# Attention rows turned by VectorE squares and DRAM instead of TensorE, and one table for the order of all later steps

## The chip, the cores and the metric

The kernel runs on one core of a Trainium2 chip. Its time is the device time of one execution in microseconds; the profile is one more execution, taken by the hardware profiler. TensorE (PE) multiplies, VectorE (DVE), ScalarE (ACT) and GpSimd (POOL) work on tiles, and all transfers are issued by SyncE (SP) to 16 DMA engines.

## What is computed

Four batches of attention with a band of 16 keys and 24 block summaries, and behind it a mixing step over the sequence and a gate of two dense layers:

```python
k_sum = k.reshape(B, H, nb, block, D).max(axis=3)      # block 32
v_sum = v.reshape(B, H, nb, block, D).mean(axis=3)
scores = concat(where(|i - j| < 16, scale * q @ k.T, -1e9), scale * q @ k_sum.T + log(block))
x = softmax(scores) @ concat(v, v_sum)                 # B, S=768, 8 heads of 64 -> 512 channels
u = x + (x.T @ U @ V).T                                # U: 768 x 32, V: 32 x 768
out = u + maximum(u @ w_ch1, 0) @ w_ch2                # 512 -> 2048 -> 512
```

## The kernel before

All products of the gate are made in three terms of high and low halves (`split`: ScalarE writes the high half, another engine the remainder). The batches are numbered 0 to 3 in the code, and the text follows that: what the title of the change calls batch 2 is index 1.

**Start.** `START` is a list of words; each is one step (a load, scores, exponentials, a turn, a value product, a mixing product). It brings batch 0's attention to the first gate product.

**Batch 0's gate** runs over f = 0..15 and two halves hf of the sequence: `up` (12 matmuls into `ps_h`, L1071), `up_out` (ScalarE writes the high half `gh`, L1083, VectorE the low half `gl`, L1084), and `down_rows` of the half before (9 matmuls into `acc`, L1093). Six PSUM banks hold `acc`; the two that are left go round between `ps_h` and everything else, so a product waits until the tile before the last has been read out. Beside it the weights come in as 64-bit floats and are converted (`turn_weights`: GpSimd L171, VectorE L177 and L180), split, summed (L923 to L927, L1050 to L1054) and stored to DRAM for the later batches. The attention of batch 1 is spread evenly over the half steps by `places`: scores (L365), masking with the row maximum on VectorE (L414) and the exponential on ScalarE (L424), `turn_half` (three transposes on TensorE into `ps_t`, L499, and a copy by ScalarE, L493), value products (`square_values`, L529), `normalise` (L541 to L543), and the mixing (`mix`, `mix_back`). `operands` then makes the seven operands of the gate: for batch 1 `mix_u` transposes the rows on TensorE (L748) and adds the mixing product in PSUM (L756); ScalarE keeps a copy.

**Batches 1 and 2** run an `up_phase` (eight p with seven products of six matmuls, L1366, after Strassen and Winograd) and a `down_phase` (16 gates f, 24 matmuls each, L1471), with `gate_high` and `gate_low` (L1439, L1443) one gate ahead. The attention of the next batch is spread over both. For batches 2 and 3 the exponentials are turned in another way: `turn_squares` (VectorE transposes 32 by 32 squares, L444), `send_squares` to DRAM (L449) and `fetch_squares` back in four loads (L457); likewise `turn_rows`, `send_rows`, `fetch_rows` for the rows (L469, L473, L482), with `add_rows` (L764, L767) in the place of `mix_u`.

**Batch 3** runs `up_phase` and `second_phase` (L1584). Weights of the later batches come back from DRAM (`fetch_weight`) and are split by `prepare` (L195 ScalarE, L196 GpSimd) right behind the product that used a unit, four units ahead. Steps of a counter (`tick`), of a queue (`drip`) and of `spread` set when each of the rest is issued.

Of the kernel before, what the change touches and what calls it, by code (L numbers as in the profile page):

```python
# [10 lines left out]
F32 = mybir.dt.float32  # L11
# [7 lines left out]
P = 128  # L19
# [16 lines left out]
VALS = 8  # L36
RING = 5
# [18 lines left out]
LEAD = 20  # L56
POOL_LOWS = ()
VALS_LENT = 6
PARTS_IN = {1: (), 2: tuple(range(NF // 2))}
AHEAD_UNITS = (45, 50)  # L60
EARLY = {7 * p + 3 : p for p in range(8)} | {7 * p + 8 : 8 + p for p in range(7)}
EARLY |= {7 * p + 13 : 16 + p for p in range(4)}
FIRST_OPERANDS = [EARLY[i] for i in sorted(EARLY)]
TURNED = {7 * p + 12 : p for p in range(6)}
# [8 lines left out]

START = """
    lm lk0 lq0 lk3 lu li lq3 X K0 Kd0 S0 K3 Kd3 E1 lk2 Xt0 lk1 S3 E0 K2 lq2 E7 Kp2 lq1 S2 E6 T6 E4
    K1 T1 F Xt1 T0 T4 Kp1 lv0 lv1 C0 lk5 S1 C6 lk6 E5 T5 lq5 E2 C1 M0 E3 T7 K5 Xt2 T2 Kp5 Mo0 Bp3 T3  # L90
    Bd2 Xs lq6 K6 C2 Dp0 C4 Dp3 lk4 Bp1 Dp1 C5 Kd6 S5 C7 V1 lk7 V4 lq4 Bp0 C3 Dp2 E10 E11 S6 V2 Xl
    K4 E12 V0 lq7 V5 V7 V3 lv2 lv3 Kp4 K7 Kp7 z0 z1 E13 S4 N1 E8 T10 V6 E9 la0 S7 T11 N2 E14 T12 la3
    T13 Q1 E15 N0 M1 Mo1 C11 N3 Bp5 I0 Bd6 T8 la1 Dd5 lr Z0 Io0 C10 Dp4 T15 lb0 Y0.0 T9 Y0.1 Bp4 Dp7
    C8 T14 V10 V11 Y0.2 C9 Dp6 la4 C14 V9 C13 Bp7 C12 N5 V8 V12 C15 N4 V13 V15 V14 N6 J0 Z1 lb1 Q0
    N7 Jo0 I2 Qo0 lb2 Io2 Y1.0 G0.0 Qo1 J2 G1.0 Y1.1 lb4 G0.1 G1.1 Go0.0 Jo2 G0.2 G0.3 W0 Go0.1
    Go1.1 G1.3 Go0.2 Go0.3 Y1.2 Go1.3 G1.2 Go1.0 Go1.2 W1 lb3 U0.0 la2 Z2
# [8 lines left out]
def body(ctx: ExitStack, tc, q0, q1, k, v, vn, uv, w1, w2, mask, ident, rep, out):  # L105
# [54 lines left out]
    def from_f64(parts, by_pool=False):  # L160

        todo = []
        for words in parts:
            n = words.shape[1] // 2
            pairs = words.rearrange("p (n w) -> p n w", w=2)
            val = mo.tile([P, DM], F32, name="val", tag="val", bufs=VALS)[:, :n]
            todo.append((pairs[:, :, 0], pairs[:, :, 1], val.bitcast(I32), val))
# [16 lines left out]
        for step in steps:  # L184
            for lo, hi, bits, _ in todo:
                step(lo, hi, bits)
                yield
        return [val for _, _, _, val in todo]
# [13 lines left out]
    def new_batch(b):  # L202
# [4 lines left out]
        st.op, st.tmp, st.h, st.rows = ({} for _ in range(4))  # L207
# [112 lines left out]
    def key_maxima(st, h):  # L320
        block_maxima(st, h)

# [1486 lines left out]
```

## Time and profile before

| | us |
|---|---|
| median of three runs | 641.9 (640.96 to 641.91) |
| the profiled execution | 636.64 |
| its span, first to last instruction | 634.7 |
| TensorE busy | 614.0 (97%) |
| VectorE busy | 443.2 (70%) |
| ScalarE, GpSimd busy | 364.0, 346.0 |
| moved by DMA | 138.46 MB |

The granted TensorE clock is 1.0 throughout. Some matmuls have two records, so counts of matmuls in the trace can be twice those in the code. A busy TensorE is modelled at the ends of matmuls, so the chain of waits is read beside it. Windows of time are used for the share of each engine in a stretch, since the stretches have different limits: start (0 to 49 us), batch 0's gate (49 to 218), batch 1's (218 to 368), batch 2's (368 to 514.5), batch 3's.

### The profile page before, as it was taken

What the parts mean: (1) busy time and instruction counts of PE and PEld (TensorE: products, weight loads), DVE (VectorE), ACT (ScalarE), POOL (GpSimd) and SP (SyncE); (2) the same over time, 40 slices, a digit from 0 to 9 for tenths busy, and PEclk for the clock granted to TensorE, in tenths of its full rate; (3) what the DMA queues carried; (4) which work ended last, traced back from release to release, by engine and by line L of the source; (5) the groups of instructions that cost most, each with busy time, mean ns of one, the idle gap of its engine ahead of it and who ended that gap; (6) DMA issues with size and microseconds to landing.
All of it is one profiled execution on the core that took longest, in us unless ns stands there. A gap on an engine that the chain in (4) does not pass through costs nothing.

```text
span 634.7 us, 14717 instructions
## 1 busy us (share of the span) xinstructions
PE 614.0 (97%) x5432; PEld 559.1 (88%) x5432; DVE 443.2 (70%) x1154; ACT 364.0 (57%) x820; POOL 346.0 (55%) x375
## 2 busy tenths in 40 slices
PE   4989999999999999999999999999999999999997
PEld 3778988889888899998888799998888889999997
DVE  4879878776888596667655764566655666756896
ACT  3865666666564556765644456675544447754552
POOL 3525977975685795782328586684134566750000
PEclk9999999999999999999999999999999999999999
DMA  9898599877687459987876366889989454366432
GB/s 235 217 385 260 161 311 295 251 235 238 177 251 216 149 156 290 266 242 241 228 235 173 103 220 181 273 249 322 278 271 270 116 179 146 117 221 235 125 119 88
DMA packets 88199, 138.46 MB, mean 218 GB/s; under 512 B 8512, under 2 KB 60096, under 8 KB 88128
## 3 DMA queue, kind: packets, MB, share of 16 engines
q1 hardware_dynamic: 88128, 137.53, 70.7%
q8 instruction: 43, 0.70, 0.5%
q14 instruction: 28, 0.23, 0.1%
HBM read 99.75 MB, written 37.75 MB: 217 GB/s over the span
## 4 chain that ended last, share of the span: by engine, by line
PE 86%; DVE 6%; SPq 2%; ACT 2%; DMA 2%; issue 2%; POOL 0%; ACTq 0%; DVEq 0%; POOLq 0%
PE ps_h L1366 27%; PE acc L1471 20%; PE acc L1093 9%; PE ps_h L1071 8%; PE accx L1584 4%; PE ps_x L529 3%; PE accy L1584 3%; PE accz L1584 3%; PE ps_s L388 2%; PE ps_s L365 2%; PE ps_t L499 2%; SPq L231 1%; DVE tmp L824 1%; DMA place<-in_v 1%; PE ps_m L714 1%
## 5 line engine op out<-in xcount | busy, mean ns | idle before, releaser
L196 POOL TENSOR_TENSOR parts<-whole,parts 128x512 fp32r<-128x512 f32 (+1 forms) x128 | 161.5, 1273 | 116.0 <-ACT parts L195 110.6
L1366 PE MATMUL ps_h<-place,parts 128*128 128x384 f32 x1008 | 181.6, 337 | 0.1
L1366 PEld LDWEIGHTS ps_h<-place,parts 128*128 128x128 f32 x1008 | 174.2, 188 | 2.5 <-issue 1.1
L1471 PE MATMUL acc<-gh,parts 128*128 128x256 f32 (+1 forms) x512 | 135.1, 342 | 0.0
L1471 PEld LDWEIGHTS acc<-gh,parts 128*128 128x128 f32 x512 | 88.9, 189 | 12.7 <-issue 1.7
L1471 PE MATMUL acc<-gl,parts 128*128 128x512 f32 (+1 forms) x256 | 86.7, 339 | 2.6 <-DVE gl L1443 2.6
L195 ACT CAST parts<-whole 128x512 fp32r<-128x512 f32 (+1 forms) x144 | 83.2, 583 | 4.1 <-issue 1.8
L424 ACT ACTIVATE e<-e,neg 128x120 f32<-128x120 f32 x144 | 46.5, 386 | 52.5 <-DVE neg L414 48.0
L1071 PE MATMUL ps_h<-place 128*128 128x384 f32 x384 | 74.6, 343 | 0.0
L1071 PEld LDWEIGHTS ps_h<-place 128*128 128x128 f32 x384 | 66.3, 188 | 1.5 <-issue 0.4
L1093 PE MATMUL acc<-place,gh 128*128 128x512 f32 x192 | 67.1, 404 | 0.0
L171 POOL TENSOR_SCALAR val<-place 128x512 f32<-128x512 f32 (+1 forms) x30 | 49.4, 1664 | 25.7 <-DMA kt<-in_k 13.3
L1471 PEld LDWEIGHTS acc<-gl,parts 128*128 128x128 f32 x256 | 48.5, 189 | 7.4 <-DVE gl L1443 3.2
L196 POOL TENSOR_TENSOR place<-val,place 128x512 fp32r<-128x512 f32 x29 | 40.6, 1419 | 17.2 <-ACT place L195 17.2
L812 POOL TENSOR_TENSOR place<-tmp,place 128x384 fp32r<-128x384 f32 x24 | 27.2, 1142 | 40.5 <-ACT place L808 35.7
L1443 DVE SCALAR_TENSOR_TENSOR gl<-place,gh 128x768 fp32r<-128x768 f32 x32 | 35.9, 1121 | 17.3 <-ACT gh L1439 16.9
L1439 ACT ACTIVATE gh<-place 128x768 fp32r<-128x768 f32 x32 | 27.0, 844 | 28.7 <-PE acc L1471 28.7
L1093 PEld LDWEIGHTS acc<-place,gh 128*128 128x128 f32 x192 | 36.1, 188 | 7.2
L414 DVE CUSTOM_DVE_ANT_0 e<-ps_s,mask_sb 128x120 f32<-128x120 f32 x144 | 32.8, 277 | 8.3 <-PE ps_s L388 5.3
L1093 PE MATMUL acc<-place,gl 128*128 128x512 f32 x96 | 37.7, 393 | 0.1
L1084 DVE SCALAR_TENSOR_TENSOR gl<-ps_h,gh 128x384 fp32r<-128x384 f32 x32 | 17.7, 554 | 23.8 <-ACT gh L1083 23.7
L1395 DVE TENSOR_TENSOR place<-place,ps_h 128x384 f32<-128x384 f32 x24 | 13.2, 551 | 30.3 <-PE ps_h L1366 30.2
(158 smaller groups left out, 1055.0 us busy)
## 6 DMA issues: line engine op xcount, KB each, us to landing
place<-in_w SPq DMA_DIRECT2D x32, 512.0 KB, 5.6
whole<-up SPq DMA_DIRECT2D x24, 512.0 KB, 4.6
whole<-up SPq DMA_DIRECT2D x24, 384.0 KB, 3.5
whole<-down SPq DMA_DIRECT2D x16, 512.0 KB, 4.8
vt<-in_v SPq DMA_DIRECT2D x48, 146.2 KB, 4.1
kt<-in_k SPq DMA_DIRECT2D x24, 288.0 KB, 5.5
there<-squares SPq DMA_DIRECT2D x16, 384.0 KB, 4.5
at<-there SPq DMA_DIRECT2D x64, 96.0 KB, 3.9
```

Source lines behind the costliest of these rows:

```text
L171: nc.gpsimd.tensor_scalar(f32(bits), f32(hi), 0.0, None, ALU.mult)
L195: nc.scalar.copy(hi, val)
L196: engine.tensor_tensor(lo, val, f32(hi), ALU.subtract)
L414: nc.vector.tensor_tensor_reduce(out=e[:, u, :], in0=ps[:, i * KC : (i + 1) * KC], in1=mask_sb[:, m, :], scale=-SCALE, scalar=BIG, op0=ALU ...
L424: nc.scalar.activation(e[:, u, :], e[:, u, :], AF.Exp, bias=st.neg[h][:, u : u + 1], scale=-1.0,)
L812: engine.tensor_tensor(by_tiles(t[:, 1]), by_tiles(val), by_tiles(f32(t[:, 0])), ALU.subtract)
L1071: nc.tensor.matmul(ps[:, :NH], w_split[0, f][:, c % 2, part_w, c // 2], ut[c], start=(n == 0), stop=(n == 3 * NC - 1),)
L1093: nc.tensor.matmul(acc[t], gt[:, sl], w_split[1, f][:, part_w], start=(first and j == 0), stop=(last and j == 2),)
L1366: nc.tensor.matmul(ps, a[:, sa, i], b[i][:, sb], start=(first and n == 0), stop=(n == 5), skip_group_check=not first,)
L1443: nc.vector.scalar_tensor_tensor(gl, h, 0.0, f32(gh), ALU.max, ALU.subtract)
L1471: nc.tensor.matmul(place, w[:, part_w, c * P : (c + 1) * P], gt[:, q0:q1], start=(f == 0 and i == 0 and j == 0), stop=(f == NF - 1 and j = ...
L1584: nc.tensor.matmul(ps, w[j][:, sa, c * P : (c + 1) * P], gate[sb], start=fresh and q == 0 and j == 0 and k == 0, stop=q == 3 and j == 1 an ...
```

## The change

Three things.

**1. Batch 1's exponentials** are no longer turned by `turn_half` but as those of batches 2 and 3: `turn_squares`, `send_squares`, `fetch_squares`. Its scores stay as they are. **2. Its rows** are turned by `turn_rows`, sent and fetched, and `operands` adds the mixing product with `add_rows`, in place (`turned = c in st.rows`). **3. The order** of all steps behind the start is read from a table, `PLAN`, which takes the place of `START`, `places`, `later`, `traffic`, `spread`, `tick` and `drip`. The table has 481 pieces, one for each point behind a group of products; a word names a step and its batch (`S1.0.1`: batch 1, head 0, bank 1 of scores; `E1.0.1.0`: masking and exponential of one tile; `T`, `s`, `f`: turn, send and fetch of a head's squares; `p0`, `p1`: ScalarE's and GpSimd's half of the next weight unit; `h`, `y`: high and low half of a gate). Steps that were one call are split into single instructions, so that the halves of `prepare`, the six maskings of a head and the parts of `operands` have places of their own. The order of the words of the start is kept, with a few words of later work put between them.

```diff
-START = """
-    lm lk0 lq0 lk3 lu li lq3 X K0 Kd0 S0 K3 Kd3 E1 lk2 Xt0 lk1 S3 E0 K2 lq2 E7 Kp2 lq1 S2 E6 T6 E4
...
+PLAN = """
+    .lm .lk0 .lq0 .lk3 .lu .li .lq3 .X .K0 .Kd0 .S0 .K3 .Kd3 .E1.0 .E1.1 .E1.2 .lk2 .Xt0 .lk1
...
+    l1.1.0 / / / v1.0 S1.0.1 E1.0.1.0 / a1.0.1 S1.0.0 d0.0 c1.3 K1.1 a1.0.1 E1.0.1.1 E1.0.1.2 t4
...
-    def turn_half(st, h, a):
-
-        transposes(st, h, a)
+    def turn_half_out(st, h, a):
+
...
-        if st.b == 1:
+        turned = c in st.rows
+        if not turned:
             mix_u(st, hf, c)
             val = st.ps_u.pop((hf, c))[:, :NH]
         else:
             add_rows(st, hf, c, kept)
             val = kept
+        if k == 0:
+            st.tmp["B12", i] = kept
+        yield
...
-        split(hi, lo, whole, nc.vector if key[0] == "second" else nc.gpsimd)
+        nc.scalar.copy(hi, whole)
         prepared.append((key, t))
...
+        def rest():
+            (nc.vector if key[0] == "second" else nc.gpsimd).tensor_tensor(lo, whole, f32(hi), ALU.subtract)
+            yield
+
+        split_next.append(rest())
...
+    plan = iter(PLAN.strip().split("/"))
+
+    def go():
+        for word in next(plan).split():
+            name = word.rstrip("0123456789.")
+            words_of[name](*map(int, filter(None, word[len(name) :].split("."))))
+
+    go()
...
             g = first.pop() if first else up_out(up(st, hf, f))
-            place(4 * f + 2 * hf)
-            traffic(f, 2 * hf)
...
+            go()
```

How the instructions of three places stand before and after. (Line numbers move with the code: L499 is gone from these places, L365 is now L452, L1071 is L1018, L1093 is L1040, L414 is L500, L1084 is L1031, L1443 is L1364, L824 is L758, L767 is L696.)

TensorE in batch 0's gate, around the product of f = 2, half 1; `ps_t<-ident_sb,e` are the transposes of batch 1's exponentials. Before:

```order
L1093 MATMUL acc_1084<-place,gl 128x512
L1093 MATMUL acc_1084<-place,gh 128x512
L499 MATMUL ps_t<-ident_sb,e 120x128 x3
L1071 MATMUL ps_h<-place 128x384 x12
L365 MATMUL ps_s<-kt,qz_85 128x120 x3
L1093 MATMUL acc_1030<-place,gh 128x512
L1093 MATMUL acc_1030<-place,gl 128x512
```

After:

```order
L1040 MATMUL acc_1098<-place,gl 128x512
L1040 MATMUL acc_1098<-place,gh 128x512
L452 MATMUL ps_s<-kt,qz_85 128x120 x3
L1018 MATMUL ps_h<-place 128x384 x12
L1040 MATMUL acc_1044<-place,gh 128x512
L1040 MATMUL acc_1044<-place,gl 128x512
```

The three transposes are gone, and scores stand where they stood.

VectorE at batch 1's first scores (`e,neg<-ps_s`: masking; `x<-val`: sums of weights; `km`: key maxima; `val`: conversion of weights). Before:

```order
L1050 TENSOR_TENSOR x<-val 128x256
L1051 TENSOR_TENSOR x<-x,val 128x256
L330 TENSOR_REDUCE km<-kt 128x3x2 x2
L177 SCALAR_TENSOR_TENSOR val<-place,val 128x512
L1084 SCALAR_TENSOR_TENSOR gl<-ps_h,gh 128x384
L414 ISA e,neg<-ps_s,mask_sb 128x120
L414 ISA neg 128x1
```

After:

```order
L272 SCALAR_TENSOR_TENSOR val<-place,val 128x512 x2
L269 SCALAR_TENSOR_TENSOR val<-place,val 128x512 x2
L1031 SCALAR_TENSOR_TENSOR gl<-ps_h,gh 128x384 x2
L500 ISA e,neg<-ps_s,mask_sb 128x120
L500 ISA neg 128x1
L997 TENSOR_TENSOR x<-val 128x256
L998 TENSOR_TENSOR x<-x,val 128x256
L417 TENSOR_REDUCE km<-kt 128x3x2 x2
```

Two low halves stand behind six conversions, and the sums and maxima have moved between the first masking of the bank and its two others, which follow right behind.

VectorE at the end of batch 1's down products; `gl` is the low half of the last gate, `x` the rows, `tmp` and `place` the operand sums of batch 2. Before:

```order
L767 TENSOR_TENSOR x_3640<-ps_u_5036,place_4818 128x3x128
L824 TENSOR_TENSOR tmp_5041<-x_3640 128x384
L824 TENSOR_TENSOR tmp_5042<-tmp_5012,x_3640 128x384
L812 TENSOR_TENSOR place_5039<-x_3640,place_5039 128x384
L1443 SCALAR_TENSOR_TENSOR gl_5053<-place_3972,gh_5052 128x768
```

After:

```order
L500 ISA e_5062,neg_5041<-ps_s_5042,mask_sb_78 128x120
L758 TENSOR_TENSOR tmp_5068<-x_3864 128x384
L500 ISA e_5062,neg_5041<-ps_s_5043,mask_sb_78 128x120
L758 TENSOR_TENSOR tmp_5077<-x_3864 128x384
L1364 SCALAR_TENSOR_TENSOR gl_5024<-place_3944,gh_5023 128x768
L758 TENSOR_TENSOR tmp_5086<-tmp_5068,x_3864 128x384
```

The four additions of rows now stand ahead of these rows, and the third operand sum behind the low half.

## Rows read from the trace of the kernel before

**Rows 1.** Page: span, and busy us (share) xinstructions of each engine.

```profile
span 634.7 us, 14717 instructions
...
PE 614.0 (97%) x5432; PEld 559.1 (88%) x5432; DVE 443.2 (70%) x1154; ACT 364.0 (57%) x820; POOL 346.0 (55%) x375
```

**Rows 2.** Chain that ended last, 64 to 92 us: start us, us, what.

```profile
66.73 0.66 PE ps_s L365 x6
67.39 2.11 PE ps_h L1071 x12
69.50 0.33 PE ps_t L499 x3
69.83 2.08 PE acc L1093 x9
```

**Rows 3.** TensorE's waits: engine line waited for: us in total, times, longest us.

```profile
PE acc L1471 <- DVE gl L1443: 2.6, 2, 1.3
...
PE ps_s L365 <- ACT kt L347: 1.3, 1, 1.3
...
PE ps_t L499 <- DVE place L812: 0.9, 1, 0.9
```

**Rows 4.** Windows: busy us (x instructions) of each engine, PEclk, DMA share, GB/s.

```profile
64.00:100.00 36.00, 36.00 (x249) 32.63 (x249) 29.32 (x81) 24.13 (x61) 30.19 (x31) 1.00 0.78 245
100.00:140.00 40.00, 40.00 (x350) 35.35 (x348) 30.59 (x89) 25.39 (x62) 31.65 (x33) 1.00 0.84 265
140.00:180.00 40.00, 39.11 (x278) 34.97 (x278) 32.39 (x69) 24.14 (x55) 26.53 (x19) 1.00 0.71 224
180.00:218.00 38.00, 37.53 (x344) 32.35 (x344) 29.42 (x60) 19.94 (x42) 25.93 (x23) 1.00 0.61 186
```

**Rows 5.** TensorE in order of time, 196 to 245 us, and the chain there.

```profile
205.33 0.33 PE ps_u L748 x3
...
218.25 3.31 PE L1366 MATMUL ps_h<-place,parts 128*128 128x384 f32 x18
```

**Rows 6.** Groups of VectorE: busy us, mean ns | idle before, releaser.

```profile
L444 DVE STREAM_TRANSPOSE squares<-e 128x768 f32<-128x768 f32 x16 | 15.5, 970 | 0.0
...
L767 DVE TENSOR_TENSOR x<-ps_u,place 128x384 f32<-128x384 f32 x16 | 8.9, 555 | 14.4 <-PE ps_u L764 14.3
```

**Rows 7.** VectorE in order of time, 354 to 370 us: start us, us.

```profile
356.26 0.56 DVE L824 TENSOR_TENSOR tmp<-x 128x384 f32<-128x384 f32 x1
...
358.56 1.57 DVE L824 TENSOR_TENSOR tmp<-x 128x384 f32<-128x384 f32 x1
```

**Rows 8.** Groups of VectorE between 64 and 218 us.

```profile
L1084 DVE SCALAR_TENSOR_TENSOR gl<-ps_h,gh 128x384 fp32r<-128x384 f32 x29 | 16.1, 555 | 23.8 <-ACT gh L1083 23.7
...
L414 DVE CUSTOM_DVE_ANT_0 e<-ps_s,mask_sb 128x120 f32<-128x120 f32 x48 | 10.9, 277 | 2.9 <-PE ps_s L365 2.9
...
L414 DVE DVE_READ_ACCUMULATOR2_ANT neg<- 128x1 f32 x48 | 4.0, 83 | 0.0
...
L330 DVE TENSOR_REDUCE km<-kt 128x6 f32<-128x192 f32 x16 | 4.8, 344 | 0.0
...
L1051 DVE TENSOR_TENSOR x<-x,val 128x256 f32<-128x256 f32 x7 | 4.8, 683 | 0.2
...
L1050 DVE TENSOR_TENSOR x<-val 128x256 f32<-128x256 f32 x7 | 3.3, 475 | 0.0
```

**Rows 9.** Groups of ScalarE.

```profile
L1083 ACT ACTIVATE gh<-ps_h 128x384 fp32r<-128x384 f32 x32 | 15.7, 491 | 30.5 <-PE ps_h L1071 30.3
```

**Rows 10.** DMA issues: queue, op xcount, KB each, median us to landing.

```profile
there<-squares SPq DMA_DIRECT2D x16, 384.0 KB, 4.5
at<-there SPq DMA_DIRECT2D x64, 96.0 KB, 3.9
```

**Rows 11.** Page, costliest groups: the low halves of weight units.

```profile
L196 POOL TENSOR_TENSOR parts<-whole,parts 128x512 fp32r<-128x512 f32 (+1 forms) x128 | 161.5, 1273 | 116.0 <-ACT parts L195 110.6 <-PE ps_h L1366 4.4
```

More of the change, by code (lines that the diff above doesn't have):

```diff
@@ L538, in normalise @@
     def normalise(st, h):
+        if not hasattr(st, "x"):
+            st.x = mo.tile([P, NU, DM], F32, name="x")
         ps = st.psx.pop(h)[:, : NU * DV].rearrange("p (u d) -> p u d", d=DV)
@@ L817, in part @@
             high(name, val)
-            low(name, val, nc.gpsimd)
+            yield
+            low(name, val, lows_by[0])
+            yield
         def tmp():
@@ L829, in operands @@
         if k == 0:
-            keep()
-            st.tmp["B12"] = kept
+            if not turned:
+                keep()
+                yield
             return
@@ L877, in scale_weights, with turned_weights, got @@
             scale_f64(words[i, f])
+    def turned_weights(k):
+        turn = turn_weights(k, True)
+        n = 3 * len(tiles(k))
+        for i in range(n):
+            next(turn)
+            if i == n - 1:
+                run(turn)
+            yield
     def turn_weights(k, by_pool=False):
-        vals = yield from from_f64([words.pop(t) for t in tiles(k)], by_pool)
-        for t, val in zip(tiles(k), vals):
-            w_val[t] = val
+        def got(vals):
+            for (i, f), val in zip(tiles(k), vals):
+                w_val[i, f] = w_kept[("down", f) if i else f] = val
+        yield from from_f64([lambda t=t: words[t] for t in tiles(k)], by_pool, got)
     def by_parts(val):
@@ L1591, in second_phase @@
                     )
+            if q == 3:
+                second_out(st, i, n, c, ps)
             yield
-            for more in range(2):
-                lead = (20 if i % 2 == 0 else -1, 6)[more]
-                while st.order and st.ready[st.order[0]] <= i and st.order[0] <= i + lead:
-                    second_operand(st, st.order.pop(0))
-                    if not more:
-                        break
-            if not st.order:
-                while st.lows:
-                    st.lows.pop()()
-            if late and i > late[0][0]:
-                finish_late()
-            if q == 3:
-                second_out(st, i + 1, n, c, ps)
-            if c == 0:
-                prepare()
-    late = []
     def finish_late():
-        _, f, *args = late.pop(0)
+        f, *args = late.pop(0)
         f(*args)
@@ new lines, in with_ends @@
+    def with_ends(ends, after, phase):
+        for i, _ in enumerate(phase):
+            yield
+            if i in after:
+                ends.pop(0)()
+                yield
+    for b in range(1, B):
+        ends = []
+        for _ in up_phase(sts[b], ends):
+            go()
+        if b in SEVEN:
+            phase = with_ends(ends, (1, 2), second_phase(sts[b]))
+        else:
+            phase = with_ends(ends, (1, 3), down_phase(sts[b]))
+        for _ in phase:
+            go()
```

730 lines of the change are left out of this document (298 added, 432 removed).

## The prediction

> **What bounds the kernel now.** I read the page's busy times first: TensorE is busy in 614.0 of 634.7 us, VectorE in 443.2, ScalarE and GpSimd in a little over half [rows 1]. A busy TensorE is not yet a bound, so the chain of waits comes next. From 64 us on (the window runs to 92) it is a string of TensorE pieces that follow each other without a gap: two score products 0.66, a gate product of twelve matmuls 2.11, three transposes 0.33, an output product of nine 2.08 [rows 2]. What is taken out of that string comes off the time, microsecond for microsecond, as long as nothing else is late. Third, TensorE's own waits: after the start they are few. 1.3 and 0.9 us fall into batch 1's work, and 2.6 us are two waits of 1.3 for a low gate half, one at the end of each middle batch [rows 3]. The change leaves the instructions of the start before the first gate product in their order on TensorE, so I count nothing there. Last, the windows from 64 to 218 us, the stretch in which batch 2's attention (index 1 in the code, "batch 1" below) rides on batch 0's products and in which nearly all of the change takes place: VectorE is busy for 29.3 + 30.6 + 32.4 + 29.4 = 121.7 of 154 us, 79%, and the DMA engines at 0.61 to 0.84 [rows 4]. That VectorE share is what the prediction hangs on.
>
> **What leaves TensorE.** Batch 1 loses 48 transposes of exponentials, 16 groups of three, at 0.33 each [rows 2]: 5.3 us. Its operands lose 24 transposes of the attention rows, 8 groups of three, also 0.33 [rows 5]: 2.6 us. Both stand in the chain back to back with products, so the whole of it is on the path: 7.9 us. The scores, the value products and the row products stay, one for one. ScalarE loses the 16 copies of turned exponentials and the 8 copies of kept rows; it is busy for 57% of the span [rows 1] and I count that at nothing, since the products hide it.
>
> The Trainium skill's page "VectorE: DVE Perf Modes", section "Rules for kernel authors", speaks against this part: it sends a 128 by 128 transpose to TensorE where a PSUM destination will do. By that rule the 7.9 us would be left where they are and this term would be 0; by the rows above it is the engine that sets the time which gives up 0.33 us a group. The rule weighs the two transposes alone, the trace says which engine is late.
>
> **What VectorE gets.** Eight turns of a head's exponentials and four turns of rows, 0.97 each [rows 6]: 11.6 us. Eight additions of the mixing product to the turned rows at 0.56 [rows 6]: 4.4. The sums behind them read the rows from SBUF and no longer from PSUM, and one of these took 1.57 where its twin took 0.56 [rows 7]; I put 1.8 us there for the whole batch (two or three such doublings; between 0 and the 12 us of twelve). Together 17.8 us in the same stretch. So VectorE would have 121.7 + 17.8 = 139.5 us of work in 154 - 7.9 = 146.1 us, 95%. This work lies beside the products, but with 6.6 us to spare it hides only if VectorE hardly waits. Before, it waited 23.8 us in this stretch for ScalarE to write the high gate half that each low half is taken from [rows 8]. The new order has to fill those waits with other work.
>
> It does so in part. The rows of VectorE at the start of batch 1 show low halves that stand behind two or three conversions of weights, so that the high half is there when VectorE arrives, but also long bursts between them. Worked out at one place: behind the product of f = 1, half 1, TensorE has scores 0.66, an output product 2.08, scores 0.66, that is 3.4 us, until the next product needs the PSUM bank of the first scores. VectorE starts its low half when ScalarE's 0.49 [rows 9] are over and has then 0.56 for it, three maskings of 0.36 with an accumulator read, sums of weights of 0.48 and 0.68 and two maxima of 0.34 to do [rows 8]: 0.49 + 0.56 + 1.08 + 1.16 + 0.68 = 4.0 us. TensorE would wait 0.6 us there, where it waits 1.3 now for key maxima on ScalarE [rows 3]. So bursts cost tenths of a microsecond each, not microseconds, while the queue stays short.
>
> What the crowding costs in all is not shown by the trace, since no stretch of it has VectorE at 95%. It can't be a gain beyond the named waits of this stretch, which are 2.2 us [rows 3], so the lower end is -2.2. The upper end is VectorE with all its old waits: 139.5 + 23.8 = 163.3 us against 146.1, 17.2 too many. The nearest rows are the windows at 140 to 180 and 180 to 218: at 81% and 77% busy they lost 0.9 and 0.5 us of TensorE [rows 4], and the two before them, at 81% and 76%, nothing. I take three times what these lost, 4.1 instead of 1.4, so **+2.7 us**.
>
> **What the DMA queues get.** SP issues 60 more transfers: 8 + 4 stores of 384 KB and 32 + 16 loads of 96 KB, 9.4 MB in all, each landing after about 4 us [rows 10]. A head then goes through masking, turn, store, load and product in some 13 us (about 3 for the maskings, 1 for the turn, 4.5, 3.9 and 1 for the product), with one buffer at each step, and a head is due every 146 / 8 = 18 us: hidden. In volume, the windows from 64 to 218 move 8.8 + 10.6 + 9.0 + 7.1 = 35.5 MB [rows 4]; 44.9 MB in 148.8 us is 302 GB/s. The window with the highest rate moved 265 GB/s at a share of 0.84 [rows 4], which is an estimated 315 GB/s at a full share. It fits, with 4% to spare; I count nothing and keep it as a rival.
>
> **What the new order does elsewhere.** Everything behind the first product is issued from one table. From 218 us on TensorE loses almost nothing but the two waits of 1.3 us [rows 3]. They come about because VectorE has operand sums in front of the low half of the last gate, one of 1.57 us [rows 7]. In the new order the high half is issued earlier on ScalarE, and two sums and two maskings stand ahead of the low half: 2 x 0.56 + 2 x 0.36 + 1.1 for the half itself, 2.9 us, while TensorE has the 24 matmuls of the gate before: twelve of 512 columns at 2.08 / 9 = 0.23 [rows 2] and twelve half as wide, 4.2 us. Both waits go: **-2.6 us**, between -2.6 and 0. Nothing else was late there, so a new order can only cost something in the rest: bounds 0 and the 17 us of the third rival, and since the spare time of the other engines is large there (VectorE at two thirds), I take a value near the lower end, **+1.5 us**.
>
> **Sum.** -7.9 + 2.7 - 2.6 + 1.5 = -6.3 us. The profiled execution, 636.6 us with a span of 634.7, would come to 630.3 with 628.4. The median of the runs shown is 641.9, 5.3 above the profiled execution; the difference is carried along: 641.9 - 6.3 = **635.6 us**. Of 0.2% (1.3 us) and more a measurement can tell the sign.
>
> **Rivals.**
> *A, VectorE becomes the bound between 64 and 218 us (slower).* The turns are done, but the low halves wait as before. Then the stretch takes 139.5 + 23.8 = 163.3 us instead of 154.0, 9.3 more, the 7.9 us of TensorE are no longer on the path, and only the two later waits are won: 641.9 + 9.3 - 2.6 = 648.6. It decides from 154.0 - 139.5 = 14.5 us of VectorE waits upwards. For it: the 95%, and the row of 1.57 us, which shows what a sum with two SBUF operands can cost beside GpSimd. Against it: the low halves have been moved behind other work.
> The Trainium skill's "GPSIMD Engine Reference", section "Specifications", says that GpSimd shares its SBUF interfaces with VectorE and that instructions with two SBUF inputs contend; the 0.56 and 1.57 us of the same sum agree with it, and by it A would be the likelier the more GpSimd does in the stretch.
> *B, the order pays in full.* No named wait behind the start is left: 641.9 - 7.9 - 2.6 - 2.2 = 629.2. For it: few waits to remove. Against it: the 95%.
> *C, weights just in time.* Before, the split of a weight unit stood four units ahead of its product everywhere; in the new table 27 of 132 units have only their own low half issued ahead. That half is a GpSimd subtraction of 1.27 us, which now waits for ScalarE 110.6 us in all without harm [rows 11]. If each of the 27 came half its length late, TensorE would lose 17 us; with half of them late 8.6: 635.6 + 8.6 = 644.2.
> *D, the trip through DRAM is late.* If the transfers of the stretch fall behind by the 5 us that the landing of one takes, weights and squares are late once or twice per batch: 635.6 + 5 = 640.6, no change.
>
> **How the numbers follow.** Forecast 0.60 (its own range 631 to 640), B 0.12, A 0.13, C 0.10, D 0.05. Faster by over 0.2%: 0.58 of the forecast, all of B, 0.02 each of C and D, 0.74. Within 0.2%: 0.02 of the forecast and of A and D, 0.03 of C, 0.09. Slower: 0.11 of A, 0.05 of C, 0.01 of D, 0.17. The range of 8 in 10 runs from 628, a little below B, to 646, which leaves out most of A.
>
> **What would show it.** In the profile after: no transposes of exponentials but those of batch 0, 24 instead of 48 of the rows; 24 and 12 turns on VectorE; batch 1's own products begin about 5 us earlier (near 213 instead of 218.25 [rows 5]) and VectorE between 64 and that point is busy for about 95%; no wait of a down product for a low half. If the first stretch is shorter by the full 7.9 us and more, my crowding was too dear; if it isn't shorter at all, A holds, and TensorE's waits there name VectorE. If the stretch is right and the time is not, the loss is in the later batches, in waits for GpSimd's halves (C) or for transfers (D). The prediction is wrong if VectorE waits over 14 us in the stretch, or if the products of the later batches wait over 5 us.

## The result, and the profile after

The changed kernel took 629.93 us (median of 4 runs, 628.68 to 630.16) against 641.43 us of the kernel before beside it: a ratio of 0.9848, 95% interval 0.9814 to 0.9883. It was compared twice more in the experiments, at 0.9865 [0.9835, 0.9895] and 0.9889 [0.9858, 0.9919]; the mean of the three is 0.987, some 8.5 us. Forecast were 635.6 us and 6.3 us less. The time lies inside the range of 628 to 646, near its lower end, below the forecast's own 631 to 640 and by rival B's 629.2.

The first two lines of the page, to be read against [rows 1] (span, then busy us, share and instructions of each engine):

```profile
span 626.9 us, 14659 instructions
...
PE 604.8 (96%) x5360; PEld 551.7 (88%) x5360; DVE 448.0 (71%) x1174; ACT 351.5 (56%) x796; POOL 338.9 (54%) x383
```

TensorE has 72 transposes fewer and is busy for 9.2 us less. VectorE has 16.0 us of turns and additions more and is busy for only 4.8 us more. The windows of the kernel after, from its first gate product (50.44) by stages to batch 1's own products (211.28) and to those of the batches behind (columns as in [rows 4]):

```profile
50.44:64.00 13.56, 13.56 (x74) 12.47 (x74) 11.93 (x23) 7.89 (x19) 7.81 (x6) 1.00 0.75 224
64.00:100.00 36.00, 34.36 (x231) 30.89 (x231) 31.78 (x88) 22.47 (x57) 26.74 (x28) 1.00 0.94 296
100.00:140.00 40.00, 39.18 (x355) 34.04 (x354) 36.31 (x87) 22.00 (x53) 30.56 (x34) 1.00 0.92 279
140.00:180.00 40.00, 40.00 (x298) 35.85 (x297) 34.99 (x89) 24.99 (x58) 25.61 (x21) 1.00 0.93 299
180.00:211.28 31.28, 31.28 (x262) 27.24 (x262) 28.86 (x55) 12.98 (x27) 22.06 (x20) 1.00 0.88 276
211.28:360.90 149.62, 148.72 (x1405) 134.17 (x1404) 104.44 (x275) 84.82 (x184) 89.51 (x108) 1.00 0.78 241
360.90:506.38 145.48, 144.08 (x1334) 130.44 (x1333) 84.16 (x240) 81.09 (x176) 76.98 (x85) 1.00 0.76 235
```

The same stages of the kernel before, with the borders where its own products begin on TensorE (49.02, 218.25, 367.84, 514.29; span 634.7), give this table, in us:

| stage | before | after | difference |
|---|---|---|---|
| start, to the first gate product | 49.02 | 50.44 | +1.42 |
| batch 0's products (the stretch) | 169.23 | 160.84 | -8.39 |
| batch 1's | 149.59 | 149.62 | +0.03 |
| batch 2's | 146.45 | 145.48 | -0.97 |
| the last batch and the end | 120.41 | 120.52 | +0.11 |
| span | 634.7 | 626.9 | -7.8 |

This places one execution of each kernel. The one of before was a short one, 636.64 us where the medians of its runs lie between 638.3 and 641.9, and two later traces of the kernel after have spans of 630.5 and 632.1. On the average of the three traces the span is 4.9 us shorter, so some 3.6 of the 8.5 us stand in no stage of these traces.

In the stretch TensorE was busy for 166.41 us before and for 158.38 after. VectorE, between 64 us and batch 1's products, has 131.9 us of work in 147.3, 90%; it had 122.0 in 154.3. TensorE's waits after the start, first in the stretch, then between 211.3 and 507 us (us in total, times, longest):

```profile
PE ps_s L452 <- ACT gh L1030: 1.4, 1, 1.4
PE ps_h L1018 <- DVE x L630: 0.7, 1, 0.7
PE ps_h L1018 <- DVE gl L1031: 0.2, 1, 0.2
...
PE ps_r L661 <- ACT t L656: 1.2, 1, 1.2
PE ps_h L1290 <- DVE o L1063: 0.8, 1, 0.8
PE ps_h L1290 <- POOL parts L968: 0.2, 1, 0.2
```

In this trace the waits of [rows 3] are gone: no down product waits for a low gate half, and neither ScalarE's key maxima nor an operand's low half holds TensorE up. Six others, 4.5 us in all, stand in their place. In the two later traces of the same kernel the last down product of batch 0 does wait for its low half, 2.0 and 1.4 us. Ahead of that low half VectorE had a sum of operands that waited 1.6 and 1.0 us for a store of weights, whose buffers (`val`) such sums share; the first of the two traces (`after_again`) has:

```profile
PE acc L1040 <- DVE gl L1031: 2.0, 1, 2.0
...
DVE tmp L758 <- DMA up<-val: 1.6, 1, 1.6
```

Groups of VectorE between 64 and 211.28 us (count, then busy us and mean ns of one, then its idle time ahead of them):

```profile
L272 DVE SCALAR_TENSOR_TENSOR val<-place,val 128x512 int32<-128x512 int32 x27 | 21.4, 807 | 0.0
L269 DVE SCALAR_TENSOR_TENSOR val<-place,val 128x512 int32<-128x512 int32 x25 | 21.1, 851 | 0.2 <-POOL val L263 0.2
L1031 DVE SCALAR_TENSOR_TENSOR gl<-ps_h,gh 128x384 fp32r<-128x384 f32 x29 | 16.0, 551 | 7.9 <-ACT gh L1030 7.5
...
L530 DVE STREAM_TRANSPOSE squares<-e 128x768 f32<-128x768 f32 x8 | 7.7, 967 | 0.0
...
L696 DVE TENSOR_TENSOR x<-ps_u,place 128x384 f32<-128x384 f32 x8 | 4.4, 548 | 1.1 <-PE ps_u L693 1.1
...
L555 DVE STREAM_TRANSPOSE place<-x 128x768 f32<-128x768 f32 x4 | 3.9, 972 | 0.1
...
L758 DVE TENSOR_TENSOR tmp<-x,tmp 128x384 f32<-128x384 f32 x2 | 1.1, 551 | 0.0
```

The turns (7.7 + 3.9) and the additions (4.4) are there at the durations of [rows 6]. VectorE waited 23.7 us for high halves before the low halves [rows 8]; it waits 7.5 now. The 13 operand sums that read the rows from SBUF take 0.55 each, but for one of 0.92; none takes 1.57 (the longest in the two later traces took 1.23 and 1.21). And the conversions of weights, the same instructions, have become shorter; before, between 64 and 218 us, they were:

```profile
L177 DVE SCALAR_TENSOR_TENSOR val<-place,val 128x512 int32<-128x512 int32 x26 | 26.0, 1000 | 0.2 <-POOL val L171 0.2
L180 DVE SCALAR_TENSOR_TENSOR val<-place,val 128x512 int32<-128x512 int32 x27 | 21.6, 837 | 0.0
```

### The profile page after: what moved, and what is told of

Same layout as the page of the kernel before. It is cut to its first block, busy times and chain, and to the rows that moved or that the text cites. A ratio compares the mean times of both kernels' runs of the same rounds, so it can differ in the third digit from the quotient of the medians.

```text
span 626.9 us, 14659 instructions
## 1 busy us (share of the span) xinstructions
PE 604.8 (96%) x5360; PEld 551.7 (88%) x5360; DVE 448.0 (71%) x1174; ACT 351.5 (56%) x796; POOL 338.9 (54%) x383
## 4 chain that ended last, share of the span: by engine, by line
PE 85%; DMA 4%; SPq 3%; DVE 3%; issue 2%; POOL 1%; ACT 1%; DVEq 0%; ACTq 0%; POOLq 0%
PE ps_h L1290 27%; PE acc L1386 19%; PE ps_h L1018 10%; PE acc L1040 9%; PE accx L1488 4%; PE accy L1488 3%; PE accz L1488 3%; PE ps_x L614 2%; PE ps_s L475 2%; DMA place<-in_q 2%; PE ps_s L452 2%; DMA there<-squares 1%; SPq L323 1%; SPq L978 1%; DMA place<-in_w 1%
## 5 line engine op out<-in xcount | busy, mean ns | idle before, releaser
L968 POOL TENSOR_TENSOR parts<-whole,parts 128x512 fp32r<-128x512 f32 (+1 forms) x128 | 158.8, 1253 | 114.4 <-ACT parts L964 98.0
L1386 PE MATMUL acc<-gh,parts 128*128 128x256 f32 (+1 forms) x512 | 134.0, 341 | 0.0
L964 ACT CAST parts<-whole 128x512 fp32r<-128x512 f32 (+1 forms) x144 | 80.4, 581 | 18.3 <-DMA whole<-dsum 5.8
L510 ACT ACTIVATE e<-e,neg 128x120 f32<-128x120 f32 x144 | 51.2, 389 | 42.5 <-DVE neg L500 39.3
L1018 PE MATMUL ps_h<-place 128*128 128x384 f32 x384 | 74.0, 341 | 1.1 <-DVE x L630 0.7
L1018 PEld LDWEIGHTS ps_h<-place 128*128 128x128 f32 x384 | 66.9, 188 | 3.8 <-issue 1.3
L1040 PE MATMUL acc<-place,gh 128*128 128x512 f32 x192 | 66.4, 400 | 0.0
L263 POOL TENSOR_SCALAR val<-place 128x512 f32<-128x512 f32 (+1 forms) x30 | 47.8, 1602 | 21.9 <-ACT place L243 14.7
L1364 DVE SCALAR_TENSOR_TENSOR gl<-place,gh 128x768 fp32r<-128x768 f32 x32 | 32.3, 1009 | 27.0 <-ACT gh L1359 27.0
L1040 PEld LDWEIGHTS acc<-place,gh 128*128 128x128 f32 x192 | 36.1, 188 | 7.2 <-ACT gh L1030 0.2
L500 DVE CUSTOM_DVE_ANT_0 e<-ps_s,mask_sb 128x120 f32<-128x120 f32 x144 | 35.1, 275 | 7.8 <-PE ps_s L452 4.4
L1040 PE MATMUL acc<-place,gl 128*128 128x512 f32 x96 | 37.9, 395 | 0.0
L530 DVE STREAM_TRANSPOSE squares<-e 128x768 f32<-128x768 f32 x24 | 23.3, 972 | 12.9 <-ACT e L510 8.4
```

The source lines that it names most:

```text
L263: nc.gpsimd.tensor_scalar(f32(bits), f32(hi), 0.0, None, ALU.mult)
L500: nc.vector.tensor_tensor_reduce(out=e[:, u, :], in0=ps[:, i * KC : (i + 1) * KC], in1=mask_sb[:, m, :], scale=-SCALE, scalar=BIG, op0=ALU ...
L510: nc.scalar.activation(e[:, u, :], e[:, u, :], AF.Exp, bias=st.neg[h][:, u : u + 1], scale=-1.0,)
L964: nc.scalar.copy(hi, whole)
L968: (nc.vector if key[0] == "second" else nc.gpsimd).tensor_tensor(lo, whole, f32(hi), ALU.subtract)
L1018: nc.tensor.matmul(ps[:, :NH], w_split[0, f][:, c % 2, part_w, c // 2], ut[c], start=(n == 0), stop=(n == 3 * NC - 1),)
```

## The experiments

Three theories stood at the start. T: what leaves TensorE comes off the time, and the new order matters only as far as it fills VectorE's waits. Against it V (the turns pay only in this order) and O (the order is what won). The first four kernels take the change apart. Each expectation is quoted as it was written ahead of the run. The ratios compare each kernel with the kernel before run beside it on the same chip.

This table gathers what the traces and times of all of them show: the first gate product, the length of the stretch (first gate product to batch 1's), TensorE's busy and idle time in it, VectorE's busy time from 64 us on with its share, and the ratio to the kernel before.

| kernel | first product | stretch | PE busy | PE idle | DVE busy | ratio, 95% interval |
|---|---|---|---|---|---|---|
| before | 49.0 | 169.2 | 166.4 | 2.8 | 122.0, 79% | 1 |
| after | 50.4 | 160.8 | 158.4 | 2.5 | 131.9, 90% | 0.9848 [0.9814, 0.9883] |
| after_again | 49.6 | 164.2 | 158.9 | 5.3 | 131.5, 88% | 0.9865 [0.9835, 0.9895] |
| after_third | 51.9 | 164.2 | 159.4 | 4.8 | 133.2, 88% | 0.9889 [0.9858, 0.9919] |
| old_order_squares | 48.8 | 168.5 | 161.9 | 6.6 | 132.7, 87% | 1.0015 [0.9988, 1.0042] |
| old_order_mended | 49.8 | 167.7 | 162.5 | 5.2 | 133.7, 87% | 0.9987 [0.9965, 1.0009] |
| rows_tensore | 50.6 | 165.5 | 161.5 | 4.0 | 125.8, 83% | 0.9934 [0.9911, 0.9957] |
| exps_tensore | 51.4 | 174.3 | 165.8 | 8.5 | 125.7, 78% | 1.0090 [1.0060, 1.0120] |
| new_order_tensore | 51.8 | 179.0 | 168.7 | 10.3 | 120.0, 72% | 1.0148 [1.0115, 1.0180] |
| turns_twice | 49.0 | 165.2 | 160.3 | 4.9 | 137.2, 91% | 0.9894 [0.9858, 0.9929] |
| turns_fourfold | 51.9 | 178.6 | 164.4 | 14.2 | 151.5, 91% | 1.0123 [1.0096, 1.0151] |
| four_moves | 49.5 | 163.9 | 159.4 | 4.5 | 130.6, 87% | 0.9827 [0.9798, 0.9856] |
| four_moves_again | 52.0 | 160.5 | 158.4 | 2.1 | 129.4, 87% | 0.9817 [0.9788, 0.9847] |
| clean_start | 53.3 | 167.4 | 160.1 | 7.3 | 134.0, 86% | 0.9957 [0.9932, 0.9982] |

### The squares in the old order

In the kernel before, one head's steps become:

```
 def turn(h, a):
-    turn_half(st, h, a)
+    if a == 0:
+        turn_squares(st, h)
+        if h >= 1:
+            fetch_squares(st, h - 1)
+    if a == (h < H - 1):
+        send_squares(st, h)
...
```

Head 7's load has a line of its own, which is not shown. The last two operand steps of the first half stand between the products of heads 6 and 7, so that head 7's trip has room.

> The kernel before, with its own planner, in which batch 1's exponentials are turned by VectorE squares and the trip through DRAM; its attention rows are still transposed on TensorE. Theory T (what leaves TensorE comes off the time in either order): 16 groups of 0.33 us go, 641.4 - 5.3 = 636.1, and the stretch from the first gate product to batch 1's own is 164 us instead of 169.2. Rival V (the turns pay only in the new order, since VectorE still waits some 23.7 us for high gate halves): VectorE has 121.7 + 7.8 + 23.7 = 153.2 us in a stretch that had 154.0, so less than 1 us is won: 640.6 or slower, and TensorE shows new waits that name VectorE.

Measured: 639.08 us, ratio 1.0015 [0.9988, 1.0042], no gain. V's forecast of no gain holds, its reason does not. TensorE lost 4.5 us of work in the stretch, and 3.8 us of it came back as waits. VectorE's waits for high halves fell from 23.7 to 11.0 us with no new order at all: they are slack that other work filled. What was lost was lost at places. TensorE's two longest waits in the stretch:

```profile
PE ps_x L529 <- DMA at<-there: 2.2, 1, 2.2
PE ps_m L721 <- DVE gl L1091: 1.8, 1, 1.8
```

The first is the trip through DRAM of one head (D's wait), the second a low half for which TensorE waited from 196.2 us on and which stood behind this (VectorE in order of time: start, us):

```profile
193.53 2.70 DVE L347 COPY kt<-km 64x48 f32<-64x48 f32 x4
196.24 1.29 DVE L180 SCALAR_TENSOR_TENSOR val<-place,val 128x512 int32<-128x512 int32 x2
197.45 0.55 DVE L1091 SCALAR_TENSOR_TENSOR gl<-ps_h,gh 128x384 fp32r<-128x384 f32 x1
```

### The exponentials back on TensorE, in the new order

In the table, each head's turn, store and load go, and two groups of transposes with ScalarE's copies come in. They stand between two pieces ahead of the place of the turn and three behind it, which for heads 3 to 6 is further ahead of the store or the load than the one or two steps that the expectation names. For example for head 3:

```
-... T1.3 ... s1.3 ... f1.3 ...
+... / H1.3.0 Ho1.3.0 / H1.3.1 Ho1.3.1 / ...
```

> The kernel after, its order kept, but batch 1's exponentials are transposed on TensorE again and copied by ScalarE, 48 transposes in 16 groups, each group one or two steps before the place where the store or the load of squares stood; rows are still turned. Theory T: 16 x 0.33 = 5.3 us come back, 629.9 + 5.3 = 635.2. Rival O (the new order is what won, the transposes would hide in it): within 1.5 us of 629.9.

Measured: 643.8 us, 1.0090. O falls: without the turns the order is slower than the kernel before. T's 5.3 us are too few, too: against the mean of the kernel after (0.987) it is 14 us. TensorE is busy for 7 us more in the stretch than in the three traces of the kernel after, and waits for 8.5 us there, most of it so:

```profile
PE ps_h L1016 <- ACT at L576: 4.1, 5, 1.4
PE ps_t L582 <- DVE gl L1029: 1.5, 3, 0.8
```

A gate product waits for ScalarE's copy out of a bank, a transpose for a low half out of another. Six of the eight PSUM banks hold batch 0's output; every other product shares two. A group of transposes takes one of them until ScalarE has copied it. The new order leaves one of these two to scores for longer, since it reads them tile by tile between other work: from the first score product of a bank to the end of its last masking it is 3.6 us on the average of batch 1's 16 banks in the kernel after, and 1.8 in the kernel before. I placed the transposes by hand, so the 14 us are a price of my places and no fair price of the order.

### The rows back on TensorE, in the new order

```
         if not turned:
             mix_u(st, hf, c)
-            val = st.ps_u.pop((hf, c))[:, :NH]
+            nc.scalar.copy(kept, st.ps_u.pop((hf, c))[:, :NH].rearrange("p (u q) -> p u q", q=P))
+            turned = True
         else:
             add_rows(st, hf, c, kept)
-            val = kept
+        val = kept
```

The words R1, r1 and g1 of all four channels leave the table.

> The kernel after, its order kept, but batch 1's attention rows are transposed on TensorE again, added to the mixing product in PSUM and copied to SBUF by ScalarE, 24 transposes in 8 groups; exponentials are still turned by squares. Theory T: 8 x 0.33 = 2.6 us come back, 629.9 + 2.6 = 632.5. Rival O: within 1 us of 629.9.

Measured: 633.74 us against 638.28 of before, 0.9934; that is 0.0067 above the mean of the kernel after, about 4 us, where T expected 2.6. TensorE is busy for 161.5 us, 2.6 more than the mean of the three traces of after (158.9). T holds for this part, within what the intervals allow; O's 1 us does not.

This kernel also gives a price of the order that needs no transposes placed by hand. It does the same work as the squares in the old order (TensorE x5384, VectorE x1162, ScalarE x804, GpSimd x383 on both pages) in the new order, and the two ran beside the same kernel before: 633.74 against 639.08 us, 0.9934 [0.9911, 0.9957] against 1.0015 [0.9988, 1.0042]. With the exponentials turned, the new order is worth about 0.8%, some 5 us. In the traces its stretch is 3.0 us shorter (165.5 against 168.5), and the old order has the two waits of 1.3 us for a low gate half that the new one lacks.

### Both back: the order alone

> The kernel after with both undone: its order, and all of batch 1's transposes on TensorE as in the kernel before. It shows what the order alone is worth. Theory T: 629.9 + 7.9 = 637.8, 3.6 us below the kernel before, of which the two waits for a low gate half are 2.6. Rival O (the order does most): 631 to 633. Rival V (the order alone is worth nothing): 641.4.

Measured: 647.58 us, 1.0148 [1.0115, 1.0180]. Both parts of the edit above in one kernel. None of the three numbers fits: this order with the old transposes, at my places, is 9 us slower than the kernel before. What this order would be worth alone, with transposes at good places, is not shown. The steps that need no such placing go one behind the other: the squares in the old order gave nothing (1.0015), the new order with them brings 0.9934, and the rows turned as well 0.987.

### The old order, mended at its two waits

The kernel with the squares in the old order, in which the load leaves `turn` and these lines change (parts left out are marked):

```
-            todo += [(first, h), (second, h)]
+            todo.append((first, h))
             if h >= 2:
                 todo.append((products, h - 2))
+            todo.append((second, h))
...
 def second(h):
+    if h >= 1:
+        fetch_squares(st, h - 1)
...
 def key_maxima(st, h):
...
-    spread_maxima(st, h, nc.vector.tensor_copy if st.b >= 2 else nc.scalar.copy)
+    spread_maxima(st, h, nc.vector.tensor_copy if st.b >= 2 and (st.b, h) != (2, 0) else nc.scalar.copy)
```

> The old order with batch 1's exponentials turned by squares, mended at the two places where TensorE waited in its trace between 180 and 200 us: the load of a head's squares is issued two steps earlier (ahead of it the product of the head before it stands one step earlier), and the spreading of batch 2's first key maxima, 2.7 us on VectorE ahead of a low half, goes to ScalarE. These places cost 2.2 and 1.8 + 0.3 us. Theory W (the turn gains its 5.3 us in any order that has no wait at these places): the stretch from the first gate product to batch 1's own shrinks from 168.5 to about 164.2 us, and the time is 4 us below the kernel before (0.993 to 0.994). Rival V (VectorE is too full in the old order, other waits take their place): no change against the kernel before, 1.000.

Measured: 637.76 against 639.03 us, 0.9987 [0.9965, 1.0009], and a stretch of 167.7 us: W fails. The trip's wait is gone and the low half's is 0.7 instead of 1.8, but what TensorE waits in the stretch only falls from 6.6 to 5.2 us. The wait for a GpSimd half of a weight grew from 0.5, and the one for key maxima of [rows 3] is still there:

```profile
PE acc L1101 <- POOL place L196: 1.4, 3, 0.7
PE ps_s L365 <- ACT kt L347: 1.3, 1, 1.3
PE ps_m L722 <- DVE gl L1092: 0.7, 1, 0.7
```

So mending the two waits that one trace showed did not bring the turn's gain; V's forecast, no change, holds here too, without VectorE being full (87%). Which places would have to be changed together in the old order stays open.

### VectorE loaded further

```
+        for _ in range(2 if st.b == 1 else 1):
             nc.vector.transpose(squares, src)
```

In the second kernel the 2 is a 4. The kernel after itself ran beside them.

> The kernel after, unchanged, beside the runs below on the same chip, so that they can be compared with it. Its ratio to the kernel before was 0.9848 [0.9814, 0.9883]; the same is expected, about 0.985. Its first gate product came at 50.4 us, 1.4 us later than in the kernel before, though no instruction of the start was changed in TensorE's order: if that is an accident of the one profile, this one comes at another time.

> The kernel after, in which each of batch 1's eight turns of exponentials on VectorE is made twice into the same squares: 8 x 0.97 = 7.8 us more for VectorE between 64 and 211 us, so 131.9 + 7.8 = 139.7 us of work in 147.3, the 95% that the prediction counted with. Theory F (VectorE's waits for high halves are slack that added work fills; it costs TensorE nothing until it is full): within 1 us of the kernel after, and VectorE's 7.5 us of waits for high halves shrink. Rival C (crowding as the prediction put it: at 95% TensorE loses 4.1 us and more, not the 2.5 it lost): 2 to 4 us above the kernel after.

> The same with each turn made four times: 24 x 0.97 = 23.3 us more for VectorE, 131.9 + 23.3 = 155.2 us of work in a stretch of 147.3. VectorE must now be the bound. Theory F: the stretch grows by the excess alone, some 8 to 10 us above the kernel after (638 to 640). Rival A (the waits stay, each turn is on the path): up to 23 us above it, 645 to 653. If it is under 4 us, VectorE has other work that moves out of the stretch.

Measured: 631.47, 632.12 and 647.25 us. Doubling the turns changes nothing that can be told: the medians lie 0.65 us apart, the ratios (0.9894 and 0.9865, each within 0.0035) 0.003. TensorE waits 4.9 us in the stretch, as in the later traces of the kernel after (5.3 and 4.8). VectorE's waits for high halves shrink from 7.0 to 4.3 us. That is what F said, but the lower end of C's 2 to 4 us lies within the intervals, and VectorE came to 91% and not to the 95% that C speaks of, so C is not tested there. The windows from 64 us to batch 1's products of the three:

```profile
64.00:213.81 149.81, 144.49 (x1137) 127.25 (x1136) 131.48 (x313) 82.74 (x194) 103.64 (x97) 1.00 0.91 284
```

```profile
64.00:214.23 150.23, 145.41 (x1136) 127.04 (x1134) 137.16 (x320) 81.86 (x193) 101.58 (x96) 1.00 0.91 279
```

```profile
64.00:230.52 166.52, 152.45 (x1155) 132.68 (x1153) 151.45 (x341) 82.36 (x195) 104.40 (x101) 0.98 0.85 260
```

Four turns in a row cost 15.8 us, between F's 8 to 10 and A's 23, though VectorE is busy for no larger share (91%) than with two. Four turns are 4.0 us in one piece, and a step of VectorE that is due behind them comes too late: behind each of the eight bursts TensorE waits for VectorE, 0.3 to 2.3 us, 11.3 of its 14.2 us of waits in the stretch, and each wait ends 0.5 to 3 us behind a burst. Elsewhere VectorE itself still waits 7.5 us for high halves, so it is not late throughout. That speaks for the burst and against the share; but no run spread the same added work in small pieces, so that VectorE is as good as full at 91% is not ruled out.

The granted clock is part of the price. It is 0.98 in this window, against 1.00 in the two others: it was at the lower of its two levels, 1.2 GHz, from 122.8 to 126.2 us and from 201.3 to 204.7, right behind waits of 2.3 and 1.8 us. Half the clock for 6.8 us is by this an estimated 3.4 of the 15.8 us. TensorE's two largest groups of waits:

```profile
PE ps_h L1019 <- DVE gl L1032: 7.5, 4, 2.3
PE ps_s L452 <- DVE gl L1032: 3.1, 3, 1.4
```

### Four steps moved

The kernel after still waits at four places for 0.7 us and more. In its table, by the number of the piece:

```
-16: x0.5 w2.0             18: S1.3.0
+16: x0.5                  18: S1.3.0 w2.0
-21: ... E1.3.1.2 U5 a1.1.0 d2.0 W0.10 t7 c1.7 c0.9 t7 P1.1 N1.1 K1.4
+21: ... E1.3.1.2 U5 a1.1.0 P1.1 N1.1 d2.0 W0.10 t7 c1.7 c0.9 t7 K1.4
-67: n1.2 U14              68: ... Us7 O1.1.3 p0 ...
+67: n1.2 U14 O1.1.3       68: ... Us7 p0 ...
-344: J3.2 R3.3 y2.12 G9 r3.3 Jo3.2 g3.2 ...     345:
+344: R3.3 y2.12 G9 r3.3 g3.2 ...                345: J3.2 Jo3.2
```

> The kernel after with four steps moved in its table, each at one of TensorE's four longest waits behind the start: the first part of a weight sum (2.8 us on VectorE) from ahead of the normalisation of head 0 to behind the next product; head 1's normalisation ahead of a down sum and two weight conversions; the last low half of an operand on GpSimd ahead of value sums; and the second mixing product of batch 3 one step later. They waited 1.4 + 0.7 + 0.8 + 1.2 = 4.1 us. If nothing else is late there: 4 us below the kernel after, about 0.65%. If the queues shift the waits elsewhere: no change, and new waits stand in their place.

> The kernel after once more, beside the next run, to settle whether the four moves gain. Expected: about 0.986 of the kernel before.

> The kernel after with the four moves, once more. If the 2.4 us that it lay below the kernel after on the last chip are real, its ratio is about 0.004 lower than that of the kernel after here too; if they were noise, the two agree within 0.002.

Measured: 629.06 us beside 631.47 of the kernel after, and 627.14 beside 631.85. The ratios are 0.9827 and 0.9817 against 0.9865 and 0.9889, so the moves gain about 0.5%, some 3.5 us: faster than both kernels. The first pair alone would not tell it (its intervals overlap), the second does. In the second trace the waits at 95, 109 and 219 us and the 1.2 us ahead of the second mixing product are gone; other waits, 2.1 us in all and the longest 0.9, stand in the stretch.

### The start cleared of batch 1's first steps

```
-0: ... K1.0 l1.0.1
-1: w0.1
-2: t2 t2 t2 k1.1 a1.0.1 t2 t2
-3: v1.1 W0.5 t3 Ka1.0 x1.1 t3 q1.1 x0.2 l1.1.0
-5:
+1: l1.0.0 k1.0 q1.0 l1.0.1 w0.1
+2: t2 t2 t2 k1.1 a1.0.1 t2 t2 a1.0.0 a1.0.0 a1.0.0
+3: v1.1 W0.5 t3 x1.1 t3 q1.1 x0.2 l1.1.0 a1.0.0 a1.0.0 a1.0.0 a1.0.0
+5: K1.0 Ka1.0
```

The seven additions a1.0.0 and the loads l1.0.0, k1.0 and q1.0 leave piece 0, the start, as well.

> The kernel with the four moves, in which the table's words for batch 1 that stand before the first gate product (two loads of value windows, head 0's keys and queries, its key maxima, and seven additions of values on GpSimd) stand behind that product, as in the kernel before. In the profiles so far the first gate product came at 48.8 to 49.8 us with the old order (three of them) and at 49.0 to 52.0, mean 50.8, with the new one (ten). Theory L (the early loads, some 0.8 MB, stand ahead of the start's own and cost it 1.5 us): first product at about 49.2, and the time 1 to 2 us below that of the four moves, a ratio of about 0.980 to the kernel before, unless batch 1's first head then comes too late. Rival N (the start varies by itself): it comes anywhere from 49 to 52, and the ratio stays at 0.982.

Measured: 636.53 us, 0.9957, 1.4% slower than the kernel that it was made from, with the first gate product at 53.3 us. Neither number fits. L falls: with the loads out of its way the start came later still, not earlier, so the first product's time is no sign of them; and N had the ratio stay. What the early steps do is another thing. Without them TensorE waits 7.3 us in the stretch, first for batch 1's first keys:

```profile
PE ps_s L448 <- ACT kt L430: 1.6, 1, 1.6
PE ps_h L1014 <- DVE neg L496: 1.3, 1, 1.3
```

The wait of 1.3 us for `kt` in [rows 3] is of this kind; the new order, which loads batch 1's first head in the start, has none in two traces of the kernel after and 0.9 us in the third. Loads, key maxima and additions moved together, so which of them counts is not separated. Why the start varies between 48.8 and 53.3 us stays open. The granted clock was 0.97 there in four of the traces, with first products at 49.5, 51.9, 51.9 and 53.3 us, and 1.00 in the others (0.97 is a mean: part of that start ran at the lower level, 1.2 GHz), so it alone does not sort them.

## Why the prediction was right, step by step, and where it was off

**What leaves TensorE, -7.9: right.** Busy time in the stretch fell by 8.0 us, and by 7.5 and 7.0 in the two later traces. The Trainium skill's page "VectorE: DVE Perf Modes", section "Rules for kernel authors", would have left the transposes on TensorE; putting the rows back there cost about 4 us, and the exponentials 14 at my places, so in the new order the runs decide for the row that said which engine is late. In the old order turning the exponentials gained nothing.

**What VectorE gets, 17.8 us and 95%: too much.** The turns and additions are exact, 16.0 us. Of the 1.8 us for sums from SBUF 0.4 came, in one sum (0.7 in each of the later traces), and the conversions of weights took 42.5 us (52 of them in the window) instead of 47.6 (53). VectorE had 131.9 us to do instead of 139.5. The weight sums took more, 37.7 us (60) instead of 34.2 (58), so these items do not add up to the difference; the rest is not worked out.

**What the crowding costs, +2.7: right in size, by a wrong road.** The step allowed TensorE 4.1 us of waits between 64 us and batch 1's products. They were 2.5, 5.3 and 4.8 in the three traces of the kernel after, 4.2 on average. But it had been reckoned from the busy share, at 95%, and the share alone does not tell it: at 91% it was 4.8 us with two turns a head and 14.1 with four. That it came out so close is luck. The step also did not count the 1.3 us for key maxima just ahead of 64 us, which went. So the stretch lost 6.2 us on the average of three traces (8.4 in the first) where 5.2 were forecast.

**Two waits for low gate halves, -2.6, and the later batches, +1.5: right.** Neither wait is left in any of the three traces; others, 2.2, 3.0 and 2.8 us in all, stand in the later batches, where 2.6 stood before. Batch 1's and batch 2's products together took 0.9 us less, where the two terms gave 1.1; in the other two traces 0.1 us more and 0.5 us less.

**The start, 0: not shown.** It was 1.4 us longer in the first trace; it varies by more than that from one execution to the next.

**The transfers, 0: right in volume.** The windows moved 276 to 299 GB/s at a share of 0.88 to 0.94; 302 had been worked out. Single transfers were late: the low half that TensorE waited for, 2.0 and 1.4 us in the later traces, stood behind a sum that waited for a store.

**The step that failed is the last line of the sum**: "the difference is carried along". The profiled execution of before was 5.3 us shorter than the median of the runs shown, and I gave the kernel after the same distance. Its own profiled execution took 628.68 us, 1.3 below its median, so 4.0 of the 5.7 us between 635.6 and 629.9 lie there, and 1.6 in the sum itself (630.3 forecast for the profiled execution). In the later comparisons the kernel before had medians of 638.3 to 639.3 us: its profiled execution was a short one, the runs shown were long ones. From 639.2, the sum's -6.3 gives 632.9 where 631.5 and 631.9 were measured. The 0.2% from which a sign was to be told were too fine as well: the intervals here reach 0.21 to 0.35% to either side.

**The rivals.** B's number was nearly met (629.2) and its mechanism was not: waits remained. A did not come; the waits that it kept are slack and fill up, to 11.0 us in the old order and 7.5 in the new. It took four turns in a row to make VectorE late again and again. C did not come: products waited 0.2 us for a GpSimd half, although 27 units have only one issued ahead. D shows in places: 2.2 us in the old order, and in the two later traces of the kernel after the 2.0 and 1.4 us behind a late store and 2.3 us of one trace in two waits for squares of the later batches.

**The signs.** Batch 1's products were to begin near 213 us; they began at 211.3, 213.8 and 216.0. One sign of being wrong did come: VectorE's waits in the stretch are 14.6 us (16.5 and 17.2 in the later traces; 31.0 before), over the 14 that the prediction named. That limit was what 139.5 us of work would have left of the stretch as it was. With 131.9 us of work there was room for more, so it was set too low and does not speak for A.

What the prediction did not say at all is that the turn's price hangs on the order. I had priced the turn and the order apart and added them up. The runs show 0 for the exponentials' turn in the old order, at two sets of places, about 5 us for the new order once they are turned, and about 4 for the rows in it. What the order is worth without the turns they do not show.

## What to carry to other kernels

An engine that waits 24 us of 154 for its operands is not thereby full: here, in the new order, 16 us of added work went into such waits, and 8 more cost nothing that could be told. Bursts of 4 us ahead of instructions that the bounding engine waits for did cost, at the same busy share. So look for the longest burst ahead of each such instruction before trusting the share. A step that takes work off the bounding engine gained only what the places around it allowed, so move the steps together with it, then read the remaining waits and move those; and compare medians with medians, since one profiled execution can lie several us beside its kernel's median.

## What the runs showed of the hardware that I had not expected

The same VectorE instruction with two SBUF inputs takes very different times. In the kernel after, a subtraction of weights (L998) took 1.52 us where its twin L1000 of the same shape took 0.38; GpSimd had begun an instruction with two SBUF inputs 0.06 us ahead of it and ended 0.28 us before it did (start, us):

```profile
104.52 1.30 POOL L288 TENSOR_TENSOR place<-val,place 128x512 fp32r<-128x512 f32 x1 [0.25 <-ACT place L287]
104.58 1.52 DVE L998 TENSOR_TENSOR x<-x,val 128x256 f32<-128x256 f32 x1
...
110.81 0.38 DVE L1000 TENSOR_TENSOR x<-val,x 128x256 f32<-128x256 f32 x1
```

The Trainium skill's page "SBUF — State Buffer", section "Who interferes with whom", says that a VectorE instruction with two SBUF inputs contends with a GpSimd instruction that reads SBUF. It also says that issue order decides who blocks. The row agrees with both, since GpSimd began first and VectorE ends 0.28 us behind it.

It follows that VectorE's work in a stretch is no fixed sum: in the windows shown the mean conversion fell from 0.90 to 0.82 us (47.6 / 53 and 42.5 / 52) though none of them was changed. The two traces bear the cause out beyond the one pair. Of the 66 conversions ahead of batch 1's own products 56 overlapped an instruction of GpSimd before and 44 after, for 48.8 and 31.8 us together; they took 0.94 and 0.87 us on average. The 10 and the 22 others took 0.69 at most. The weight sums of 128x256 went the other way: all 64 together overlapped GpSimd for 27.8 us before and 30.3 after and took 37.9 and 39.8 us, and those that overlapped nothing took 0.43 at most. GpSimd's spans are rough in a profile, and no run changed this overlap alone.
